# One chunk transposed by DMA, and the stages around it put in another order

## The chip, the cores and the metric

One NeuronCore of a Trainium2 chip. The metric is the device time of one execution in microseconds, as the median of several. Where I say *span*, I mean the time from the first to the last instruction in the profile; the metric is about 1.8 to 2.2 us longer than the span, and that rest is not in the trace.

## The reference, cut to what matters

```python
def _A_ref(x, wqkv, wo):            # sliding window attention, 32 heads of 16, window 8, dilation 2
    qkv = (x @ wqkv)...             # q, k, v
    logits = einsum(q, k[window]) * scale ; attn = softmax(logits)
    o = einsum(attn, v[window])
    return o.reshape(B, S, D) @ wo

def _B_ref(x, w1, w2, w3, w4):      # shifted token mixer and an MLP
    h = gelu(layernorm(x) @ w1)
    x1 = x + shifted(h) @ w2
    return x1 + gelu(layernorm(x1) @ w3) @ w4

xn = layernorm(A_x)                 # S = 2048, D = 512, F = 1376, bf16
out = A_x + _A_ref(xn) * silu(_B_ref(xn))
```

## The kernel before

The 2048 rows are split by parity into two halves of 1024, and each half into two chunks of 512 rows: chunk 0 and 1 are parity 0, chunk 2 and 3 parity 1. Each chunk is normalised on VectorE (DVE), transposed, and then feeds q/k, v and (after a second scaling) w1. `stage_t` transposes half a chunk by TensorE, with a copy out of PSUM (the memory in banks that TensorE writes its results to) behind it; `stage_r` and `stage_m` spread a factor per row over the chunk and multiply it in; `ln_again` makes that factor, with the last step (a power) on GpSimd (POOL). SP is the engine that only issues DMAs, here the *head-row moves* (`spread`), which copy rows of q and k to where the scores read them. The whole order is fixed by hand: each engine executes its instructions in the order in which these calls stand.

```python
    def ln_norm(c):
        p, k = c // 2, c % 2
        x_c = xn[p][:, k * TPC : (k + 1) * TPC, :]
        for lo, hi, mv, rstd in lns[c]:
            for j in range(lo, hi):
                nc.vector.tensor_scalar(
                    out=x_c[:, j, :], in0=x_c[:, j, :], scalar1=mv[:, j - lo, 0:1],
                    scalar2=rstd[:, j - lo : j - lo + 1], op0=ALU.subtract, op1=ALU.mult,
                )

    def ln_again(c):
        r2 = small.tile([P, TPC], F32, name="r2", tag="r2")
        eng = nc.vector if c == 3 else nc.gpsimd
        for lo, hi, mv, rstd in lns[c]:
            r = r2[:, lo:hi]
            eng.tensor_tensor(out=r, in0=rstd, in1=rstd, op=ALU.mult)
            eng.tensor_tensor(out=r, in0=r, in1=mv[:, :, 1], op=ALU.mult)
        eng.tensor_scalar(out=r2, in0=r2, scalar1=EPS, scalar2=None, op0=ALU.add)
        r2b = small.tile([P, TPC], BF16, name="r2b", tag="r2b")
        with nc.allow_low_precision("bf16 factors"):
            nc.gpsimd.tensor_tensor(out=r2b, in0=r2, in1=nhalf, op=ALU.pow)
    ...
    def stage_t(c, h):
        p, k = c // 2, c % 2
        x_c = xn[p][:, k * TPC : (k + 1) * TPC, :]
        pt = pst("wb"[h % 2], "tr_ps").bitcast(BF16)[:, 0, :].rearrange("p (a j q) -> p a j q", a=ND, j=2)
        for j in range(2):
            jj = 2 * h + j
            for dt in range(ND):
                nc.tensor.transpose(pt[:, dt, j, :], x_c[:, jj, dt * P : (dt + 1) * P], ident[:])
        t0 = k * CH + 2 * h * P
        copy = nc.vector.tensor_copy if c == 1 and h else nc.scalar.copy
        copy(out=xnT[p][:, :, t0 : t0 + 2 * P], in_=pt.rearrange("p a j q -> p a (j q)"))
    ...
    def stage_m(c):
        p, k = c // 2, c % 2
        cs = slice(k * CH, (k + 1) * CH)
        rrep = xn2T[c][:, ND - 1, :]
        nc.vector.tensor_tensor(
            out=xn2T[c], in0=xnT[p][:, :, cs], in1=rrep.unsqueeze(1).to_broadcast([P, ND, CH]), op=ALU.mult
        )
```

The order from chunk 2 on, and the attention units of parity 0 with the w2 and q/k tiles between their scores:

```python
    ...
    ln_stats(2)
    ln_again(2)
    stage_w1(0, 1)
    mask_fill(0)
    spread(0, 0, CH)
    ln_norm(2)
    for a in range(2):
        qk_pair(1, a)[0]()
    stage_r(1)
    stage_m(1)
    for a in (2, 3):
        qk_pair(1, a)[0]()
    stage_x()
    stage_t(2, 0)
    stage_t(2, 1)
    ln_stats(3, 0, 2)
    ln_stats(3, 2, 4)
    ln_norm(3)
    ln_again(3)
    stage_w1(1, 0)
    stage_w1(1, 1)
    stage_r(2)
    stage_m(2)
    qk_pair(2, 0)[0]()
    stage_t(3, 0)
    stage_t(3, 1)
    qk_pair(2, 1)[0]()
    stage_w1(2, 0, lambda: stage_r(3))
    stage_m(3)
    mask_fill(1)
    spread(0, CH, X)
    stage_w1(2, 1)
    load_w3()
    stage_w1(3, 0)
    stage_w1(3, 1)
    va = values(0, 0)
    ...
    w2q = [lambda t=t: w2_and(t) for t in range(S // P)]
    qkq = [lambda t=t: qk_one(2 + t // 8, t % 8) for t in range(4, 16)]
    for n, (a, b) in enumerate(
        (("www", "qq"), ("q", "ww"), ("qw", "qw"), ("q", "ww"), ("qw", "qw"), ("q", "ww"), ("qw", "qw"), ("q", "w"))
    ):
        for i, x in enumerate((a, b)):
            for y in x:
                groups[n][i].append((w2q if y == "w" else qkq).pop(0))
    ...
    def attend(n):                  # one attention unit, cut
        prs = [scores(p, u, 0)]     # two PSUM tiles s, t; exp of each on ScalarE
        out = weighted(*prev)       # previous unit: probabilities times values, PSUM tile o
        for f in groups[n][0]: f()  # q/k and w2 tiles, PSUM tiles w, b in turn
        nva = values(*order[n + 1])
        out()                       # DVE casts tile o
        prs.append(scores(p, u, 1))
        for f in groups[n][1]: f()
```

The softmax here doesn't subtract the row's maximum and nothing guards it: scores larger than these inputs give would overflow.

Of the kernel before, what the change touches and what calls it, by code (L numbers as in the profile page):

```python
# [15 lines left out]
def kernel(  # L16
# [14 lines left out]
    nc = tc.nc  # L31
    P = 128
# [11 lines left out]
    CH = 512  # L44
    NCH = S // CH
    TPC = CH // P
# [65 lines left out]
    rr_at = (184, 75)  # L112
    sg_at = (61, 66, B0 + 33.5)

    cnt = {"v": 0, "p": 1, "b": 0, "r": 0, "g": 0}

    def pst(tag, name):
        return psum.tile([P, 2 if tag in "sto" else 1, CH], F32, name=name, tag=tag)
# [114 lines left out]
    def mask_full(w):  # L233
        nc.vector.tensor_tensor(
            out=mask[:, w, :].rearrange("p (g s l) -> p g s l", s=2, l=W),
            in0=gk[:, w, :].rearrange("p (g s) -> p g s", s=2).unsqueeze(3).to_broadcast([P, 32, 2, W]),
            in1=edge[:, w].unsqueeze(1).to_broadcast([P, 32, 2, W]), op=ALU.add,
        )

    def mask_fill(k):  # L240
        for w in range(2):
            for e in range(2):
                for a, b, m in ((0, CH, 0),) if k == 0 else ((CH, CH + 480, 32), (CH + 480, X, 32)):
                    nc.vector.tensor_copy(
                        out=(kT, qT)[w][e][:, :, a:b],
                        in_=mask[:, w, m : m + b - a].unsqueeze(1).to_broadcast([P, ND, b - a]),
                    )

    def spread(p, lo, hi, q=nc.sync, ws=(0, 1)):
        for w in ws:  # L250
            for e in range(2):
                for gr in range(4):
                    r = 32 * gr + DH * e
                    q.dma_start(
                        out=(kT, qT)[w][e][r : r + DH, :, lo:hi], in_=kq[p][w][r : r + DH, :, lo:hi]
                    )
# [32 lines left out]
    lns = {}  # L289

    def ln_stats(c, lo=0, hi=TPC):
        p, k = c // 2, c % 2
        lns.setdefault(c, []).append((lo, hi, *layer_stats(xn[p][:, k * TPC : (k + 1) * TPC, :], "l1", lo, hi)))
# [26 lines left out]
            nc.tensor.transpose(pt[:, dt, :], xn[0][:, j, dt * P : (dt + 1) * P], ident[:])  # L320
        nc.scalar.copy(out=xnT[0][:, :, j * P : (j + 1) * P], in_=pt)  # L321

    def ln_norm(c):
        p, k = c // 2, c % 2
        x_c = xn[p][:, k * TPC : (k + 1) * TPC, :]
        for lo, hi, mv, rstd in lns[c]:
            for j in range(lo, hi):
                nc.vector.tensor_scalar(
                    out=x_c[:, j, :], in0=x_c[:, j, :], scalar1=mv[:, j - lo, 0:1],
# [14 lines that stand above are left out]
        r2s[c] = r2b  # L344
# [9 lines that stand above are left out]
        t0 = k * CH + 2 * h * P  # L354
        copy = nc.vector.tensor_copy if c == 1 and h else nc.scalar.copy
        copy(out=xnT[p][:, :, t0 : t0 + 2 * P], in_=pt.rearrange("p a j q -> p a (j q)"))

    def stage_x():
        nc.gpsimd.tensor_copy(out=xnT[1][:, :, M:X], in_=xnT[0][:, :, M - DW : M])

    def stage_r(c):
        rp = psb("rrep_ps")
        r2 = r2s.pop(c)
        for j in range(TPC):
            nc.tensor.matmul(
                rp[:, j * P : (j + 1) * P], lhsT=r2[:, j : j + 1].to_broadcast([P, P]), rhs=ident[:],
                start=True, stop=True,
            )
        nc.scalar.copy(out=xn2T[c][:, ND - 1, :], in_=rp)
# [8 lines that stand above are left out]
# [4 lines left out]
    def qk_pair(c, a, halves=1):  # L382
        p, k = c // 2, c % 2
        pt = psa("qk_ps")
        w = CH // halves

        def part(hh):
            for b in range(2):
                nt = 2 * a + b
                for dt in range(ND):  # L390
                    nc.tensor.matmul(  # L391
                        pt[:, b, hh * w : (hh + 1) * w], lhsT=wqk_sb[:, dt, nt * P : (nt + 1) * P],
                        rhs=xnT[p][:, dt, k * CH + hh * w : k * CH + (hh + 1) * w],
                        start=(dt == 0), stop=(dt == ND - 1),
                    )
            if hh == halves - 1:
                dst, n0 = qk_dst(p, 2 * a)
                nc.scalar.copy(out=dst[:, n0 : n0 + 2, k * CH : (k + 1) * CH], in_=pt)
                if c == 1:
                    nc.scalar.copy(out=dst[:, n0 : n0 + 2, M:X], in_=pt[:, :, CH - DW : CH])  # L400

        return [lambda hh=hh: part(hh) for hh in range(halves)]
# [13 lines left out]
    def stage_w1(c, a, mid=None):  # L416
        p, k = c // 2, c % 2
        pt = psa("w1_ps")
        for b in range(2):
            g = 2 * a + b  # L420
            if b and mid:
                mid()
            for dt in range(ND):
                nc.tensor.matmul(  # L424
                    pt[:, b, :], lhsT=w1_sb[:, dt, g * P : (g + 1) * P], rhs=xn2T[c][:, dt, :],
                    start=(dt == 0), stop=(dt == ND - 1),
                )
        nc.scalar.activation(
            hT[p][:, 2 * a : 2 * a + 2, 1 + k * CH : 1 + (k + 1) * CH], pt, AF.Gelu_apprx_tanh
        )  # L430
# [100 lines left out]
    def values(p, u):  # L531
        q0, nq, k0, nk = units[u]
        va = v_aug[cnt["v"] % NV]
        cnt["v"] += 1
        vp = psb("v_ps")
        for dt in range(ND):
            nc.tensor.matmul(  # L537
                vp[:nk, :], lhsT=xnT[p][:, dt, k0 : k0 + nk], rhs=wv_sb[:, dt, :],
                start=(dt == 0), stop=(dt == ND - 1),
            )  # L540
        nc.vector.tensor_copy(  # L541
            out=va[:nk, :, 0:DH], in_=vp[:nk, :].rearrange("p (h d) -> p h d", d=DH)
        )
        return va
# [179 lines left out]
    stage_r(0)  # L724
    stage_m(0)
    ln_norm(1)
    mask_full(0)
    mask_full(1)
    parts[1][1]()
    parts[2][1]()  # L730
    qk_pair(0, 3)[0]()
    stage_w1(0, 0)
    stage_t(1, 0)
    stage_t(1, 1)
    ln_stats(2)
    ln_again(2)
    stage_w1(0, 1)
    mask_fill(0)
    spread(0, 0, CH)
    ln_norm(2)  # L740
    for a in range(2):
        qk_pair(1, a)[0]()
    stage_r(1)
    stage_m(1)
    for a in (2, 3):
        qk_pair(1, a)[0]()
    stage_x()
    stage_t(2, 0)
    stage_t(2, 1)
    ln_stats(3, 0, 2)  # L750
    ln_stats(3, 2, 4)
    ln_norm(3)
    ln_again(3)
    stage_w1(1, 0)
    stage_w1(1, 1)
    stage_r(2)
    stage_m(2)
    qk_pair(2, 0)[0]()
    stage_t(3, 0)
    stage_t(3, 1)  # L760
    qk_pair(2, 1)[0]()
    stage_w1(2, 0, lambda: stage_r(3))
    stage_m(3)
    mask_fill(1)
# [1 line left out]
    stage_w1(2, 1)  # L766
    load_w3()
    stage_w1(3, 0)
    stage_w1(3, 1)
    va = values(0, 0)  # L770

    groups = {n: ([], []) for n in range(len(order))}
# [3 lines left out]
        w2_tile(c, j)  # L776

    w2q = [lambda t=t: w2_and(t) for t in range(S // P)]
    qkq = [lambda t=t: qk_one(2 + t // 8, t % 8) for t in range(4, 16)]
    for n, (a, b) in enumerate(  # L780
        (("www", "qq"), ("q", "ww"), ("qw", "qw"), ("q", "ww"), ("qw", "qw"), ("q", "ww"), ("qw", "qw"), ("q", "w"))
    ):
        for i, x in enumerate((a, b)):
            for y in x:
                groups[n][i].append((w2q if y == "w" else qkq).pop(0))
# [8 lines left out]
    st3(2, 2, 3)  # L794
    late[3] += [lambda: ln3_norm(0), lambda: normalise_dn(0, 0), lambda: ln3_turn(0)]
    st3(3, 4)
    st3(4, 5, 6, 7)
    late[6] += [lambda: ln3_norm(1), lambda: normalise_dn(0, 1), lambda: ln3_turn(1)]

    w4s = [w4_tile(t) for t in range(S // P)]  # L800
# [31 lines left out]
    late[N1 + 7].append(lambda: normalise_end(1, 0))  # L832
    CUT = 480
    for w in range(2):
        late[3 + w].append(lambda w=w: spread(1, 0, CUT, nc.gpsimd, (w,)))

    prev = None

# [121 lines left out]
```

## Time and profile before

| | before |
|---|---|
| time, median of 3 | 206.55 us (206.49 to 206.68) |
| span of the profiled run | 204.8 us |
| TensorE busy | 197.3 us, 96% of the span |
| first group of matmuls that takes over 0.1 us too long after 10.4 us | the scores that begin at 50.75 us (0.21 us) |
| sum of the late starts from 43.6 to 90.8 us | 1.85 us |

The lines behind the table stand in the prediction. The last two rows are not in any view: they come from the list of matmul starts in the trace, as the distance from one start to the next less the usual one for its shape (216 ns for 128x512, 56 ns for a transpose, 312 ns from a 128x512 matmul to the first one of the scores). What is late is noted at the start of the group of matmuls that takes too long by it, so 57.74 stands for a group whose successor starts 0.24 us late, at 58.84. Where one engine is busy for 96% of the span, this list is the measure that counts: an engine that looks busy may still start an instruction late, and only a late start is time that a change of order can win.

### The profile page before, as it was taken

How to read it: one execution, taken by the hardware profiler on the slowest of the kernel's cores; microseconds unless marked ns; L12 is line 12 of the kernel's file. 1: busy time of each engine (PE TensorE's matmuls, PEld its weight loads, DVE VectorE, ACT ScalarE, POOL GpSimd, SP SyncE). 2: the span in 40 equal slices, each digit the busy share in tenths (PEclk: the TensorE clock that was granted, in tenths of full speed). 3: DMA queues.
4: the chain of work that ended last, by engine and by line, in shares of the span. 5: the costliest groups of instructions: out<-in, count | busy, mean ns of one | idle time of the engine just before them, and what ended most of it. 6: DMA issues, size and time to landing. Idle time of an engine off the chain costs nothing.

```text
span 204.8 us, 4854 instructions
## 1 busy us (share of the span) xinstructions
PE 197.3 (96%) x1944; PEld 95.6 (47%) x1944; DVE 135.2 (66%) x256; ACT 132.7 (65%) x160; POOL 74.1 (36%) x145
## 2 busy tenths in 40 slices
PE   7799999999999999999999999999999999999990
PEld 2475455444444444544444444444455544444440
DVE  5788996545487986776940001188577968888693
ACT  2366788868968687885556557898788877212130
POOL 4798465000032294933791000003830590700000
PEclk9999999999999999999999999999999999999999
DMA  5992065067900399485779948695130241554312
GB/s 131 361 349 84 15 101 96 0 97 113 293 10 0 108 121 151 86 212 105 180 178 215 286 145 134 93 254 193 34 54 3 52 92 26 122 162 135 95 51 77
DMA packets 30590, 25.69 MB, mean 125 GB/s; under 512 B 12505, under 2 KB 28481, under 8 KB 30569
## 3 DMA queue, kind: packets, MB, share of 16 engines
q1 hardware_dynamic: 28376, 22.17, 43.0%
q0 software_dynamic: 2048, 3.09, 8.9%
q8 instruction: 15, 0.25, 0.5%
q10 hardware_dynamic: 144, 0.13, 0.2%
q14 instruction: 7, 0.05, 0.1%
HBM read 12.40 MB, written 4.46 MB: 82 GB/s over the span
## 4 chain that ended last, share of the span: by engine, by line
PE 87%; ACT 4%; DVE 4%; POOL 1%; DMA 1%; issue 1%
PE w_ps L511 19%; PE w_ps L491 19%; PE qk_ps L391 8%; PE v_ps L537 7%; PE w_ps L424 7%; PE s_ps L557 6%; PE w_ps L447 6%; PE wo_ps L673 6%; PE o_ps L580 4%; PE qk_ps L409 4%; ACT arena L562 3%; PE tr_ps L353 1%; DMA arena<-in_A_x_dram 1%; ACT arena L414 1%; DVE l0s L304 1%; POOL l0r L308 1%
## 5 line engine op out<-in xcount | busy, mean ns | idle before, releaser
L562 ACT ACTIVATE arena<-s_ps 128x960 bf16<-128x960 f32 (+1 forms) x68 | 62.9, 979 | 14.4 <-PE s_ps L557 14.4
L511 PE MATMUL w_ps<-arena 128*128 128x512 bf16 (+1 forms) x164 | 39.1, 380 | 0.0
L496 ACT ACTIVATE arena<-w_ps 128x1024 bf16<-128x1024 f32 x20 | 20.5, 1023 | 15.0 <-PE w_ps L491 14.3
L491 PEld LDWEIGHTS <-arena 128*128 128x128 bf16 (+1 forms) x176 | 17.5, 100 | 20.6 <-issue 0.4
L622 POOL DMA_DIRECT2D arena<-orw x48 | 24.9, 527 | 5.8 <-DVE orw L592 5.8
L511 PEld LDWEIGHTS <-arena 128*128 128x128 bf16 (+1 forms) x176 | 16.5, 98 | 19.6
L683 POOL TENSOR_TENSOR arena<-arena 128x512 bf16<-128x512 bf16 x6 | 7.7, 1301 | 44.5 <-DVE arena L681 44.5
L526 ACT ACTIVATE sig<-arena 128x512 bf16<-128x512 bf16 x16 | 10.1, 630 | 20.8 <-DVE arena L517 20.7
L541 DVE CAST v_aug<-v_ps 128x512 bf16<-128x512 f32 x17 | 11.7, 688 | 14.6 <-PE v_ps L537 14.6
L592 DVE CAST orw<-o_ps 128x960 bf16<-128x960 f32 (+1 forms) x17 | 19.7, 1156 | 2.5 <-PE o_ps L580 2.4
L491 PE MATMUL w_ps<-arena 128*128 128x512 bf16 (+1 forms) x88 | 19.5, 379 | 0.1
L491 PE MATMUL w_ps<-arena,arena 128*128 128x512 bf16 (+1 forms) x88 | 19.2, 379 | 0.0
L391 PE MATMUL qk_ps<-arena 128*128 128x512 bf16 (+1 forms) x104 | 18.6, 330 | 0.5 <-ACT arena L321 0.5
L537 PE MATMUL v_ps<-wv_sb,arena 128*128 128x512 bf16 x68 | 17.5, 380 | 0.1
L557 PEld LDWEIGHTS <-arena 32*128 32x128 bf16 x544 | 10.1, 92 | 14.5 <-issue 14.4
L273 POOL TENSOR_SCALAR l3r<-l3m 128x1 f32<-128x1 f32 (+1 forms) x10 | 2.2, 222 | 39.0 <-DVE l3m L282 39.0
L557 PE MATMUL s_ps<-arena 32*128 32x120 bf16 (+1 forms) x544 | 15.8, 214 | 0.0
L447 PE MATMUL w_ps<-arena 128*128 128x512 bf16 x64 | 15.7, 380 | 0.1
L517 DVE TENSOR_TENSOR arena<-w_ps,arena 128x512 bf16<-128x512 f32 x16 | 11.0, 686 | 7.2 <-PE w_ps L511 7.2
L650 DVE TENSOR_TENSOR arena<-arena,orw 128x1440 bf16<-128x1440 bf16 (+1 forms) x2 | 1.6, 784 | 20.5 <-DMA orw<-rden_d 20.5
L424 PE MATMUL w_ps<-arena 128*128 128x512 bf16 x64 | 14.6, 379 | 0.0
L451 DVE TENSOR_TENSOR arena<-w_ps,arena 128x512 bf16<-128x512 f32 x16 | 10.7, 686 | 4.1 <-PE w_ps L447 4.1
(98 smaller groups left out, 278.9 us busy)
## 6 DMA issues: line engine op xcount, KB each, us to landing
x1n_dram<-arena SPq DMA_DIRECT2D x4, 512.0 KB, 3.0
arena<-in_A_x_dram SPq DMA_DIRECT2D x4, 512.0 KB, 6.1
arena<-in_A_x_dram SPq DMA_DIRECT2D x6, 256.0 KB, 7.0
out_dram<-arena SPq DMA_DIRECT2D x6, 256.0 KB, 3.0
arena<-in_B_w_dram SPq DMA_DIRECT2D x1, 1376.0 KB
arena<-in_B_w_dram SPq DMA_DIRECT2D x1, 1280.0 KB
arena<-arena SPq DMA_DIRECT2D x16, 72.0 KB, 2.6
arena<-arena SPq DMA_DIRECT2D x16, 68.0 KB, 3.5
```

Of the source, the lines that this page charges most:

```text
L391: nc.tensor.matmul(pt[:, b, hh * w : (hh + 1) * w], lhsT=wqk_sb[:, dt, nt * P : (nt + 1) * P], rhs=xnT[p][:, dt, k * CH + hh * w : k * CH ...
L424: nc.tensor.matmul(pt[:, b, :], lhsT=w1_sb[:, dt, g * P : (g + 1) * P], rhs=xn2T[c][:, dt, :], start=(dt == 0), stop=(dt == ND - 1),)
L447: nc.tensor.matmul(pt, lhsT=w2_src(p, g, m0), rhs=w2_sb[:, g, :], start=(g == 0), stop=(g == ND - 1))
L491: nc.tensor.matmul(pt[:fs, ft % 2, :], lhsT=w3_sb[:, dt, ft * P : ft * P + fs], rhs=x1nT[c][:, dt, :], start=(dt == 0), stop=(dt == ND - 1),)
L496: nc.scalar.activation(h3(c, 2 * a, 2), pt, AF.Gelu_apprx_tanh)
L511: nc.tensor.matmul(pt, lhsT=h3(c, ft, 1)[:fs, 0, jj * P : (jj + 1) * P], rhs=w4_sb[:fs, ft, :], start=(ft == 0), stop=(ft == NF - 1),)
L537: nc.tensor.matmul(vp[:nk, :], lhsT=xnT[p][:, dt, k0 : k0 + nk], rhs=wv_sb[:, dt, :], start=(dt == 0), stop=(dt == ND - 1),)
L557: nc.tensor.matmul(st[:nk, b, i * nq : (i + 1) * nq], lhsT=kT[e][r : r + 32, dt, k0 : k0 + nk], rhs=qT[e][r : r + 32, dt, q0 : q0 + nq], s ...
L562: nc.scalar.activation(prv[:nk, 2 * h : 2 * h + 2], st[:nk, :, 0 : 4 * nq], AF.Exp, scale=SCALE)
L592: nc.vector.tensor_copy(out=orw[p, r][:, :, :, q0 - ra : q0 - ra + nq], in_=op[:, :, 0 : 4 * nq].rearrange("p j (s q) -> p j s q", q=nq),)
L622: nc.gpsimd.dma_start(out=oT[p][DH * hh : DH * (hh + 1), :, ra : ra + rw], in_=orw[p, r][32 * cg : 32 * cg + DH, jj],)
L673: nc.tensor.matmul(pt, lhsT=oT[p][:, dt, i * P : (i + 1) * P], rhs=wo_sb[:, dt, :], start=(dt == 0), stop=(dt == ND - 1),)
```

## The change

Intent: take chunk 2's transposes off TensorE by sending the chunk to DRAM and back through a DMA transpose; norm chunk 3 in halves so that its own transposes can fill the time until the data is back; issue the moves of head rows of parity 0 in parts, so that SP's queue is free for the store and the transpose; load ScalarE's exp table before the first scores; and take three q/k tiles out of the attention units so that these become alike. Cut to its core:

```diff
+    def turn_dma(c, lo=0, hi=TPC):
+        p, k = c // 2, c % 2
+        rows = x1n_dram[c * CH + lo * P : c * CH + hi * P, :]
+        nc.sync.dma_start(
+            out=rows.rearrange("(i q) d -> q i d", q=P), in_=xn[p][:, k * TPC + lo : k * TPC + hi, :]
+        )
+        return lambda: nc.sync.dma_start_transpose(
+            out=xnT[p][:, :, k * CH + lo * P : k * CH + hi * P], in_=rows
+        )
...
     ln_norm(1)
-    mask_full(0)
-    mask_full(1)
     parts[1][1]()
     parts[2][1]()
     qk_pair(0, 3)[0]()
+    ln_stats(2, 0, 2)
     stage_w1(0, 0)
     stage_t(1, 0)
     stage_t(1, 1)
-    ln_stats(2)
+    ln_stats(2, 2, 4)
+    mask_full(0)
+    ln_norm(2)
+    turn_dma(2)()
     ln_again(2)
     stage_w1(0, 1)
-    mask_fill(0)
-    spread(0, 0, CH)
-    ln_norm(2)
+    mask_full(1)
+    mask_fill(0, (0,))
     for a in range(2):
         qk_pair(1, a)[0]()
     stage_r(1)
     stage_m(1)
+    ln_stats(3, 0, 2)
+    spread(0, 0, CH, nc.sync, (0,))
     for a in (2, 3):
         qk_pair(1, a)[0]()
     stage_x()
-    stage_t(2, 0)
-    stage_t(2, 1)
-    ln_stats(3, 0, 2)
     ln_stats(3, 2, 4)
-    ln_norm(3)
-    ln_again(3)
+    ln_norm(3, slice(0, 1))
     stage_w1(1, 0)
     stage_w1(1, 1)
     stage_r(2)
+    stage_t(3, 0)
+    ln_norm(3, slice(1, 2))
     stage_m(2)
+    ln_again(3)
     qk_pair(2, 0)[0]()
-    stage_t(3, 0)
     stage_t(3, 1)
     qk_pair(2, 1)[0]()
+    mask_fill(0, (1,))
+    spread(0, 0, CH, nc.sync, (1,))
     stage_w1(2, 0, lambda: stage_r(3))
...
     stage_w1(3, 0)
+    qk_pair(2, 2)[0]()
     stage_w1(3, 1)
+    qk_one(2, 6)
+    nc.scalar.preload_act_table_set("exp_and_others")
     va = values(0, 0)
...
-    qkq = [lambda t=t: qk_one(2 + t // 8, t % 8) for t in range(4, 16)]
+    qkq = [lambda t=t: qk_one(2 + t // 8, t % 8) for t in range(7, 16)]
     for n, (a, b) in enumerate(
-        (("www", "qq"), ("q", "ww"), ("qw", "qw"), ("q", "ww"), ("qw", "qw"), ("q", "ww"), ("qw", "qw"), ("q", "w"))
+        [("www", "qw")] + [("q", "ww")] * 6 + [("q", "q")]
     ):
```

Left out: the parameters that let `ln_norm`, `mask_fill` and `spread` do a part; the start of the PSUM rotation (`"p": 0` for 1, since one more tile is taken); one statistics step moved a unit on; and the second head-row move of parity 1, one attention unit later (unit 5 for unit 4).

More of the change, by code (lines that the diff above doesn't have):

```diff
@@ L113 @@
     sg_at = (61, 66, B0 + 33.5)
-    cnt = {"v": 0, "p": 1, "b": 0, "r": 0, "g": 0}
+    cnt = {"v": 0, "p": 0, "b": 0, "r": 0, "g": 0}
     def pst(tag, name):
@@ L238, in mask_full, with mask_fill @@
         )
-    def mask_fill(k):
-        for w in range(2):
+    def mask_fill(k, ws=(0, 1)):
+        for w in ws:
             for e in range(2):
@@ L247, in mask_fill, with spread @@
                     )
-    def spread(p, lo, hi, q=nc.sync, ws=(0, 1)):
+    def spread(p, lo, hi, q=nc.sync, ws=(0, 1), es=(0, 1)):
         for w in ws:
-            for e in range(2):
+            for e in es:
                 for gr in range(4):
@@ L321, in first_t, with ln_norm @@
         nc.scalar.copy(out=xnT[0][:, :, j * P : (j + 1) * P], in_=pt)
-    def ln_norm(c):
+    def ln_norm(c, part=slice(None)):
         p, k = c // 2, c % 2
         x_c = xn[p][:, k * TPC : (k + 1) * TPC, :]
-        for lo, hi, mv, rstd in lns[c]:
+        for lo, hi, mv, rstd in lns[c][part]:
             for j in range(lo, hi):
@@ L796 @@
     st3(3, 4)
-    st3(4, 5, 6, 7)
+    st3(4, 5, 6)
+    st3(5, 7)
     late[6] += [lambda: ln3_norm(1), lambda: normalise_dn(0, 1), lambda: ln3_turn(1)]
@@ L834 @@
     for w in range(2):
-        late[3 + w].append(lambda w=w: spread(1, 0, CUT, nc.gpsimd, (w,)))
+        late[3 + 2 * w].append(lambda w=w: spread(1, 0, CUT, nc.gpsimd, (w,)))
     prev = None
```

## The prediction

> **What bounds the kernel now.** I read the page first: who is busy, and when.
>
> ```profile
> PE 197.3 (96%) x1944; PEld 95.6 (47%) x1944; DVE 135.2 (66%) x256; ACT 132.7 (65%) x160; POOL 74.1 (36%) x145
> PE   7799999999999999999999999999999999999990
> PEclk9999999999999999999999999999999999999999
> PE 87%; ACT 4%; DVE 4%; POOL 1%; DMA 1%; issue 1%
> ```
>
> TensorE is busy from the third slice to the last but one, at full granted clock; every other engine has a third of its time free. Busy matmuls can hide waits, so next I took the matmul starts from the trace and read the distance from each to the next. A 128x512 matmul takes 216 ns, a transpose 56 ns, in nearly every case. From 10.4 us to 43.6 us not one matmul starts late: the two load stages before it and the tail after 198.1 us, both untouched by the change, are the only large holes. Then the chain of waits in order of time (start, duration, what), around the three chunks that are still transposed by TensorE:
>
> ```profile
> 17.98 0.89 PE tr_ps L353 x16
> ...
> 27.73 0.89 PE tr_ps L353 x16
> 28.62 3.45 PE w_ps L424 x16
> 32.08 0.22 PE rrep_ps L365 x4
> 32.30 1.73 PE qk_ps L391 x8
> 34.03 0.89 PE tr_ps L353 x16
> ```
>
> The line at 27.73 is chunk 2: 16 transposes back to back, 0.89 us, on the path. The 1.73 at 32.30 is the first reader of the transposed chunk.
>
> From 43.6 us to 90.8 us (the first eight attention units beside the w2 and q/k tiles) there are small stalls. Beyond the normal slots I count: 0.21 at 50.75, 0.14 at 53.70, 0.24 at 57.74, about 0.17 each at 61.97, 67.02, 73.00, 78.05 and 84.03, 0.05 and 0.07 at 68.96 and 79.97, 0.29 at 87.25; 1.85 us in all. The ScalarE timeline there:
>
> ```profile
> 45.05 1.28 ACT L562 ACT_TABLE_LOAD   x1 [0.15 <-PE s_ps L557]
> 46.35 1.94 ACT L562 ACTIVATE arena<-s_ps 128x1024 bf16<-128x1024 f32 x2
> 49.00 1.94 ACT L562 ACTIVATE arena<-s_ps 128x1024 bf16<-128x1024 f32 x2 [0.72 <-PE s_ps L557]
> 50.83 1.08 ACT L414 CAST arena<-qk_ps 128x512 bf16<-128x512 f32 x2
> 51.77 1.88 ACT L562 ACTIVATE arena<-s_ps 128x960 bf16<-128x960 f32 x2
> ```
>
> The exp table load does not stall TensorE: ScalarE still idles 0.72 us before the second pair of exps. What backs ScalarE up a little is the pair of q/k casts at 50.83.
>
> **What the skill says.** "TensorE: Matmul & The Clock Gate", Part 4, gives a 128x128 bf16 transpose about 390 ns alone and about 275 ns in one kernel. This trace disagrees: 16 of them leave every 56 ns, so chunk 2 costs 0.89 us and not 4.4, and I use 0.89. "DMA: Bandwidth & Descriptors", DMA Transpose (X-bar), says a DMA transpose needs HWDGE and an SBUF destination, and that two streams of them at once corrupt each other; the before kernel sends four, all from SP, and the new one joins that queue, so it is legal. "ScalarE: Activation LUTs", What ACT_TABLE_LOAD costs, has 1283 ns plus a drain of 1380 ns; the trace shows the 1283 ns, but exp starts 0.02 us after the load ends, so I count no drain. "SBUF — State Buffer" says DVE and GpSimd share a port pair by an exclusive lock; the trace agrees in kind: the same 128x2 tensor_scalar on POOL takes 0.23 us at 13.21 and 1.20 us at 14.24, when DVE runs the 128x2048 multiply.
>
> **The change, part by part.**
>
> *Chunk 2 by DMA.* Removes 16 transposes: -0.89 us on the path, and two 128x1024 copies (about 1 us each) from ScalarE, which is not the bound there. It adds a 512 KB store and a DMA transpose. Both have rows in the before kernel:
>
> ```profile
> 69.22 0.40 SPq L473 DMA_DIRECT2D x1n_dram<-arena  x1
> 69.72 0.62 SPq L614 DMA_DIRECT2D dn<-den_d  x1
> 72.21 2.63 SPq L478 DMA_TRANSPOSE arena<-x1n_dram  x1
> DMA to landing us min/median/max: 4.3/4.6/5.0
> ```
>
> 3.0 us for the store, 4.3 to 5.0 for the transpose, 7.3 to 8.0 together. When can it start? DVE ends the norm of chunk 1 at 17.0; two stats pairs of 1.6 us with the 0.7 us copy of chunk 1 between them end near 21.1; POOL is free of its memset at 20.4 and needs 0.23 + 0.73 us per half for the rstd, the second half slowed by the lock; the four norms (1.4 us) end at 23.8 to 24.3. It lands at 31.1 to 32.3, estimated from those rows. The first reader comes at 32.14 in matmul starts, less 0.89, plus 0.45 for the half of chunk 3's transposes now ahead of it: 31.70. So the landing straddles the need; I put 0.2 us of stall there (0 to 0.8).
>
> *Norm of chunk 3 in halves.* No work added. It lets transposes of half 0 go ahead of q/k, which buys the DMA the 0.45 us above. DVE: the multiply of chunk 1 can start at 25.8 (ScalarE's cast of the factors) and must end by 27.57, when w1 of chunk 1 starts; I estimate 27.0 to 27.3. Then two stats pairs, and half 0's norm ends near 31.2 against 31.25. The factor of chunk 3 needs POOL's power (1.04 to 1.85 us) after DVE at about 34.8, while DVE now fills masks beside it: ready at 35.9 to 37.1, needed at about 36.5 to 36.7. I put 0.2 us for all of these.
>
> *Head-row moves in parts.* 32 SP issues of about 0.6 us, the same number; only their times move. Part 1 is behind the transpose, to about 34.6 us; part 2 starts after its fill at about 36, takes 8 x 0.645 = 5.2 us to issue and lands near 43.7. First scores: 44.57 - 0.89 + 1.73 + 0.86 (three q/k tiles moved ahead) = 46.3. Some 2.5 us to spare: nothing.
>
> *Tiles and the table.* Three q/k tiles leave the attention units for the stage before: the same 12 matmuls, 2.6 us either way. The later units become alike (one q/k tile, then two w2 tiles). The stalls at 57.74, 68.96 and 79.97 are values waiting for the bank of a q/k tile whose cast sits behind two exps; with no w2 tile between, these 0.36 us go, and the 0.14 at 53.70 too as only one cast is behind the first unit. The 0.17 before each next unit's scores stays: two 216 ns x 4 groups (1.83 us) are shorter than two exps (1.83 us plus start), and one unit that had none will get it. Net -0.33. The table load moves into the shadow of values: first exp some 0.7 us nearer to its scores, worth 0 on the path.
>
> Sum: -0.89 + 0.2 + 0.2 - 0.33 = -0.82; 206.55 becomes about 205.7. I shade it to 205.6, since the halves look placed on purpose to avoid just these stalls.
>
> **Rivals.** (1) *The DMA lands late.* The path norm, store, transpose has no slack by my count, and each us past 31.7 is a us on TensorE. For: the before run shows 5.0 us under traffic. Against: the input loads have all landed by 17.3 us in the trace, and SP's moves are queued behind it, so the engines are empty. At 1.5 us late: 206.9. (2) *All hidden, everything in time.* Then 0.89 and 0.33 are both kept, plus perhaps some of the 0.17s: 205.3, at best 204.8. (3) *ScalarE becomes the bound in the attention units*, through one cast per unit: 2 x 1.83 + 0.59 = 4.3 us against 5.05 us of TensorE. Against it: that ratio; the time would not move by more than 0.3. (4) *The DMA transpose frees nothing since TensorE waits for DVE anyway*: against it, the slots show no wait from 10.4 to 43.6.
>
> **Range and chances.** Gains are capped by 0.89 + 1.85 us, which would be 203.8 with every stall gone; 2% would be 202.4, so faster by 2% needs work that the change does not remove. Slower by 2% needs 4 us of lateness in a path that I estimate at most 1 or 2 us late. Range 204.8 to 206.5.
>
> **What would show it right or wrong.** After: 32 transposes at the stage's line in place of 48; store issued at 23.5 to 24.5 us and transpose landed by 31.1 to 32.3; a TensorE gap under 0.8 us before the first q/k of chunk 2, small ones before the factor matmuls of chunk 3; w3 starting about 0.8 us earlier than 88.41; span after w3 unchanged. The prediction is wrong if the transpose takes much over 5 us, if the norm of chunk 2 ends after 25 us, if the moves of part 2 land after the first scores, or if the stalls between units grow.

## The result, and the profile after

Ratios in this document are the mean time of one kernel's fast runs over that of the other's of the same rounds, so not quite the ratio of the medians that stand beside them.

| | before | after |
|---|---|---|
| time, median of 6 | 206.57 us (206.49 to 206.68) | 206.01 us (205.92 to 206.29) |
| ratio | | 0.9974 (95%: 0.9962 to 0.9987) |
| span of the profiled run | 204.8 us | 204.1 us |

The change makes the kernel 0.54 us faster (0.0026 x 206.57), a quarter of a per cent. The page of the kernel after, by engine, by slice and by the chain:

```profile
PE 195.2 (96%) x1900; PEld 94.9 (47%) x1928; DVE 135.0 (66%) x256; ACT 131.5 (64%) x157; POOL 74.5 (37%) x149
PE   7899999999999999999999999999999999999990
PE 71%; DVE 11%; DMA 9%; issue 3%; POOL 3%; ACT 2%; SPq 0%; DVEq 0%; POOLq 0%
```

TensorE is still busy for 96% of a span that is a little shorter. Two things here mislead. The count of matmuls fell by 44 where the change removes 16: the weight loads fell by exactly 16 (from 1944 to 1928), so 28 matmul records are missing, and the busy time of this line is low by a little. And the share of TensorE in the chain fell from 87% to 71% although nothing changed behind 87.73 us: the last stage takes 72.29 us in both kernels. At the end the chain now runs back over DMAs that landed at nearly the same time as the work beside them. A chain is one path, and where two are about as long, which of them is shown is chance.

What did change stands in SP's queue and in the chain from 31 us on. SP's timeline of the kernel after (start, duration, what):

```profile
23.29 0.39 SPq L361 DMA_DIRECT2D x1n_dram<-arena  x1
26.28 1.41 SPq L364 DMA_TRANSPOSE arena<-x1n_dram  x1
27.81 23.05 SPq L254 DMA_DIRECT2D arena<-arena  x32
```

The store goes out at 23.29 us, the transpose 2.99 us later, when the store has landed. The last of the transpose's completion records is at 31.11 us, 4.83 us after its issue; the first q/k of chunk 2 starts at 31.49 us. So the DMA is in time, by 0.38 us. The chain of the kernel after, next:

```profile
32.62 1.22 DVE arena L385
34.63 0.44 issue
35.07 1.58 POOL r2b L343
36.70 0.40 PE rrep_ps L375 x4
37.09 4.10 PE w_ps L434 x19
```

Here the chain leaves TensorE. The four matmuls at 36.70 spread the factors of chunk 3, and they wait for POOL's power, which starts at 35.07 and takes 1.58 us. By the list of starts they come 0.44 us late; the profile of before has no such gap.

A table of stages tells the rest. Stage 1 runs from the first transpose of chunk 1 (17.6 to 17.9 us) to the first scores, stage 2 from there to the first w3 matmul, stage 3 (38.72 us in every kernel) over w3, stage 4 from the first scores of parity 1 to the last matmul. Where the three q/k tiles are moved, I put their 12 matmuls (12 x 0.216 = 2.59 us) back into stage 2, so that all rows compare.

| kernel | stage 1 | stage 2 | stage 4 | mean span of the fast runs | time less span |
|---|---|---|---|---|---|
| before | 26.76 | 43.84 | 72.29 | 204.76 | 1.78 |
| after | 26.31 | 43.80 | 72.29 | 204.18 | 1.86 |
| e1 front only | 26.32 | 43.83 | 72.58 | 204.52 | 2.03 |
| e2 tiles only | 26.76 | 43.48 | 72.29 | 204.38 | 2.14 |
| e3 no preload | 26.31 | 43.80 | 72.29 | 204.32 | 1.85 |
| e4 again first | 25.86 | 43.80 | 72.29 | 203.98 | 1.87 |
| e5 turn on PE | 27.21 | 43.48 | 72.29 | 204.80 | 2.24 |
| e6 late norm | 26.96 | 43.80 | 72.29 | 204.90 | 1.87 |
| e7 no half ahead | 26.31 | 43.79 | 72.29 | 204.26 | 1.85 |
| e8 split w2 | 25.86 | 47.15 | 72.30 | 207.25 | 1.87 |
| e9 ACT plus 2 | 26.31 | 43.49 | 72.29 | 203.83 | 1.88 |
| e10 ACT plus 1 | 26.31 | 43.49 | 72.59 | 204.08 | 1.85 |
| e11 split, late cast | 25.86 | 43.65 | 72.29 | 203.57 | 1.84 |
| e12 e4 and e9 | 25.86 | 43.49 | 72.29 | 203.48 | 1.88 |

Stages are from the profiled execution of each kernel, and they repeat to 0.01 us between kernels that share the code, which makes them a finer measure than the time. Stage 1 gained 0.45 us, and stage 2, where I had counted on 0.33, gained 0.04.

### The profile page after: what moved, and what is told of

Same layout as the page of the kernel before. It is cut to its first block, busy times and chain, and to the rows that moved or that the text cites. A ratio compares the mean times of both kernels' runs of the same rounds, so it can differ in the third digit from the quotient of the medians.

```text
span 204.1 us, 4800 instructions
## 1 busy us (share of the span) xinstructions
PE 195.2 (96%) x1900; PEld 94.9 (47%) x1928; DVE 135.0 (66%) x256; ACT 131.5 (64%) x157; POOL 74.5 (37%) x149
## 4 chain that ended last, share of the span: by engine, by line
PE 71%; DVE 11%; DMA 9%; issue 3%; POOL 3%; ACT 2%; SPq 0%; DVEq 0%; POOLq 0%
PE w_ps L501 19%; PE w_ps L521 10%; PE v_ps L547 8%; PE s_ps L567 7%; PE w_ps L457 6%; PE qk_ps L401 5%; PE w_ps L434 5%; PE o_ps L590 4%; PE qk_ps L419 4%; DMA den_d<-orw 3%; PE wo_ps L683 3%; DMA arena<-rden_d 2%; DVE arena L537 2%; DMA rden_d<-rb 1%; DVE arena L691 1%
## 5 line engine op out<-in xcount | busy, mean ns | idle before, releaser
L521 PE MATMUL w_ps<-arena 128*128 128x512 bf16 (+1 forms) x156 | 38.5, 380 | 0.6 <-issue 0.2
L401 PE MATMUL qk_ps<-arena 128*128 128x512 bf16 (+1 forms) x109 | 20.4, 332 | 0.5 <-ACT arena L321 0.3
L501 PE MATMUL w_ps<-arena 128*128 128x512 bf16 (+1 forms) x86 | 19.4, 379 | 0.2
L527 DVE TENSOR_TENSOR arena<-w_ps,arena 128x512 bf16<-128x512 f32 x16 | 11.0, 686 | 7.9 <-PE w_ps L521 7.9
L457 PE MATMUL w_ps<-arena 128*128 128x512 bf16 x63 | 15.2, 380 | 0.1
L434 PE MATMUL w_ps<-arena 128*128 128x512 bf16 x63 | 14.6, 379 | 0.0
L401 PEld LDWEIGHTS <-arena 128*128 128x128 bf16 x112 | 10.6, 98 | 7.9 <-DMA arena<-in_A_wqkv_dram 0.8
```

Source lines behind the costliest of these rows:

```text
L401: nc.tensor.matmul(pt[:, b, hh * w : (hh + 1) * w], lhsT=wqk_sb[:, dt, nt * P : (nt + 1) * P], rhs=xnT[p][:, dt, k * CH + hh * w : k * CH ...
L434: nc.tensor.matmul(pt[:, b, :], lhsT=w1_sb[:, dt, g * P : (g + 1) * P], rhs=xn2T[c][:, dt, :], start=(dt == 0), stop=(dt == ND - 1),)
L457: nc.tensor.matmul(pt, lhsT=w2_src(p, g, m0), rhs=w2_sb[:, g, :], start=(g == 0), stop=(g == ND - 1))
L501: nc.tensor.matmul(pt[:fs, ft % 2, :], lhsT=w3_sb[:, dt, ft * P : ft * P + fs], rhs=x1nT[c][:, dt, :], start=(dt == 0), stop=(dt == ND - 1),)
L521: nc.tensor.matmul(pt, lhsT=h3(c, ft, 1)[:fs, 0, jj * P : (jj + 1) * P], rhs=w4_sb[:fs, ft, :], start=(ft == 0), stop=(ft == NF - 1),)
```

## The experiments

All twelve gave correct results, and each has four to six timed runs beside the kernel before (206.54 to 206.61 us there).

### e1: the front of the change alone

The kernel after with the loop, the q/k tiles, the table load and the PSUM start of before.

```diff
-    qk_pair(2, 2)[0]()
     stage_w1(3, 1)
-    qk_one(2, 6)
-    nc.scalar.preload_act_table_set("exp_and_others")
...
+        (("www", "qq"), ("q", "ww"), ("qw", "qw"), ...            # the loop of before
```

> Front part of the change alone (chunk 2 by DMA, norm of chunk 3 in halves, head-row moves in parts); q/k tiles, exp table and loop as in the kernel before. Theory T (read from the trace after): 0.89 us of transposes gone, 0.44 us given back at the factor matmuls of chunk 3, the DMA itself in time: -0.45 us against before, about 206.1. Rival R1 (the front keeps its full 0.89 and the loss is elsewhere): 205.7. Rival R2 (the gain comes from tiles and table, the front is a wash): 206.5.

Measured: 206.57 us, ratio 0.9999 (0.9986 to 1.0013). The time did not move, but stage 1 is 26.32 us, 0.44 less than before, as Theory T had it. Two things ate it: stage 4 is 0.29 us longer (e10 comes back to that), and 0.25 us more lies outside the span (2.03 against 1.78).

### e2: tiles and table alone

The opposite half: the kernel before with the moved tiles, the early table and the new loop.

> Moved q/k tiles, early exp table and the regular loop alone, chunk 2 still transposed on TensorE. Theory T (the stalls of the attention units sum to 1.76 us after against 1.85 us before): -0.1 us against before, about 206.45. The prediction's term: -0.33, about 206.2. Rival R2: -0.5, about 206.0.

Measured: 206.45 us, ratio 1.0000 (0.9987 to 1.0012). Stage 2 is 43.48 us: 0.36 us less than before, the prediction's term and not the one that I had read from the trace after. In the time it does not show, since 0.36 us more lies outside the span. By mean spans the halves nearly add up: -0.24 (e1) and -0.38 (e2) against -0.57 for the whole. That is luck: e1 loses 0.29 us in stage 4, which the whole does not, and the whole has 43.80 us in stage 2: with the front in place, 0.32 us of this half are lost again.

### e3: without the early table

```diff
-    nc.scalar.preload_act_table_set("exp_and_others")
```

> The changed kernel without the early exp table; the load then happens at the first exp. Theory T: ScalarE has over 1 us free before the second pair of exps in the first unit, so the same time as after within 0.1 us. Rival (the load sits on the path): up to 1.28 us slower than after.

Measured: 206.15 us, ratio 0.9983 (0.9970 to 0.9995); all stages as after. ScalarE's timeline, first of the kernel after, then of e3:

```profile
46.48 1.28 ACT L785 ACT_TABLE_LOAD   x1
47.77 1.94 ACT L572 ACTIVATE arena<-s_ps 128x1024 bf16<-128x1024 f32 x2
50.95 1.94 ACT L572 ACTIVATE arena<-s_ps 128x1024 bf16<-128x1024 f32 x2 [1.24 <-PE s_ps L567]
```

```profile
47.11 1.28 ACT L572 ACT_TABLE_LOAD   x1 [0.54 <-PE s_ps L567]
48.41 1.94 ACT L572 ACTIVATE arena<-s_ps 128x1024 bf16<-128x1024 f32 x2
51.06 1.94 ACT L572 ACTIVATE arena<-s_ps 128x1024 bf16<-128x1024 f32 x2 [0.72 <-PE s_ps L567]
```

The early load brings the first exp forward by 0.53 us (0.64, less 0.11 by which the whole run of e3 is later), and ScalarE's idle time before the second pair grows by as much, from 0.72 to 1.24 us. The load was hidden before, and hiding it better is worth nothing.

### e4: the factors of chunk 3 first

```diff
-    stage_m(2)
     ln_again(3)
+    stage_m(2)
```

> The changed kernel with the factors of chunk 3 computed on DVE before the multiply of chunk 2, so that POOL's power is not held up behind DVE's multiply and mask fills. Theory T (the 0.44 us TensorE gap in front of the factor matmuls of chunk 3 is this wait and nothing else takes its place): 0.3 to 0.45 us faster than after, about 205.6. Rival: POOL is blocked by DVE's mask fills just as long, or w1 of chunk 2 then waits for its later multiply: no change.

Measured: 205.80 us, ratio 0.9967 (0.9955 to 0.9980); stage 1 is 25.86 us, 0.45 less than after. TensorE's timeline of the kernel after, then POOL's of the same kernel:

```profile
35.39 1.03 PE L434 MATMUL w_ps<-arena 128*128 128x512 bf16 x4
36.70 0.40 PE L375 MATMUL rrep_ps<-ident,r2b 128*128 128x128 bf16 x4 [0.28 <-POOL r2b L343]
```

```profile
35.07 1.57 POOL L343 TENSOR_TENSOR r2b<-r,nhalf 128x4 bf16<-128x4 f32 x1 [3.84 <-DVE r L340]
```

The same two of e4:

```profile
35.65 1.03 PE L434 MATMUL w_ps<-arena 128*128 128x512 bf16 x4
36.52 0.39 PE L375 MATMUL rrep_ps<-ident,r2b 128*128 128x128 bf16 x4
```

```profile
33.48 1.90 POOL L343 TENSOR_TENSOR r2b<-r,nhalf 128x4 bf16<-128x4 f32 x1 [1.99 <-DVE r L340]
```

In e4 the power is done at 35.38 us, over a microsecond early, and four w1 matmuls and the factor matmuls follow without a gap (35.65 + 4 x 0.216 = 36.51). It even takes longer there, 1.90 us; it starts while DVE's multiply runs, and whether that is the reason was not tested. So the gap after is the power's late start: in the changed order DVE makes its input only behind the multiply of chunk 2. (POOL starts 0.49 us after DVE's last step ended, in e4 0.48, where DVE's mask fills do not run yet; so nothing shows that the fills set that start.)

### e5: chunk 2 on TensorE again

```diff
-    turn_dma(2)()
...
     stage_x()
+    stage_t(2, 0)
+    stage_t(2, 1)
```

> The changed kernel with chunk 2 transposed by TensorE again, all else as after. Theory T: +0.89 us of transposes, but the factor matmuls of chunk 3 come 0.89 us later and their 0.44 us wait goes: +0.45 us against after, about 206.45. Rival R1 (the transposes cost their full time): +0.89, about 206.9. Rival (the transposes were hidden): 0.

Measured: 207.05 us, ratio 1.0023 (1.0010 to 1.0035). Stage 1 is 27.21 us, 0.90 more than after: Rival R1. The wait before the factor matmuls of chunk 3 did not go. TensorE's timeline of e5, the same two lines as in e4:

```profile
36.37 1.03 PE L434 MATMUL w_ps<-arena 128*128 128x512 bf16 x4
37.67 0.40 PE L375 MATMUL rrep_ps<-ident,r2b 128*128 128x128 bf16 x4 [0.28 <-POOL r2b L343]
```

From 36.37 to 37.67 are 1.30 us, as from 35.39 to 36.70 in after: 0.44 more than four matmuls take. The transposes stand ahead of the factor matmuls of chunk 2, and behind those runs the path that the wait ends: ScalarE's cast, DVE's multiply (at 33.59 us for 32.62), DVE's input of the power, the power (at 36.04 for 35.07). All of it moves with TensorE, so the wait keeps its length. My reading that the transposes' removal had *brought* this wait was wrong: it belongs to the order of `stage_m` and `ln_again`, and it costs the same with the transposes and without. The DMA is worth its full 0.90 us in this order. (Stage 2 is 0.32 us shorter here, and 0.38 us more lies outside the span than after.)

### e6: the DMA 1.5 us later

```diff
-    ln_norm(2)
-    turn_dma(2)()
-    ln_again(2)
-    stage_w1(0, 1)
     mask_full(1)
     mask_fill(0, (0,))
+    ln_norm(2)
+    turn_dma(2)()
+    ln_again(2)
+    stage_w1(0, 1)
```

> The changed kernel with the second mask table and the first fill (0.68 + 1.29 us of DVE) put ahead of the norm of chunk 2, so that its store and DMA transpose start about 2 us later. The transpose landed at 31.1 us after and was needed at 31.5. Theory T (slack of 0.4 us): TensorE waits about 1.6 us before the first q/k of chunk 2, less the 0.44 us of the later wait: +1.1 to +1.6 us against after. Rival (the DMA has much slack, or DVE's and POOL's order shifts the rest): under +0.3.

Measured: 206.75 us, ratio 1.0009 (0.9997 to 1.0022); stage 1 is 0.65 us longer than after. The store goes out at 24.79 us, 1.50 us later and not 2, since the norm now runs without a wait for POOL in its middle. TensorE's timeline of e6:

```profile
31.12 0.61 PE L353 MATMUL tr_ps<-ident,arena 128*128 128x128 bf16 x8
32.67 1.89 PE L401 MATMUL qk_ps<-arena 128*128 128x512 bf16 x7 [0.94 <-ACT arena L379]
36.57 1.03 PE L434 MATMUL w_ps<-arena 128*128 128x512 bf16 x4
37.43 0.39 PE L375 MATMUL rrep_ps<-ident,r2b 128*128 128x128 bf16 x4
```

The eight transposes end their slots at 31.12 + 0.45 = 31.57, and q/k starts at 32.67: 1.10 us late. The named releaser (a ScalarE cast, of the factors of chunk 2) is not what it waited for: in after the same q/k starts at 31.49 us, before this cast, which begins at 32.01 there. The transpose's last completion record is at 32.53 us, 1.42 us later than after. Against TensorE's own stream, which runs 0.08 us later as a whole in this run, that is 1.34 us later; less the 1.10 of waiting it leaves 0.24 us of slack. After has 0.38 us between record and start, and here a start follows its record by 0.14 us: 0.24 again. And since the factor matmuls now come later than the power, their 0.44 us are gone (36.57 + 0.86 = 37.43): 1.10 - 0.44 = 0.66, measured 0.65. That lies between the two expectations: Theory T had the mechanism, but a delay of 2 us for 1.50. Its slack of 0.4 us was nearer to 0.24.

### e7: no half of chunk 3 ahead

```diff
     stage_r(2)
-    stage_t(3, 0)
     ln_norm(3, slice(1, 2))
     stage_m(2)
     ln_again(3)
     qk_pair(2, 0)[0]()
+    stage_t(3, 0)
     stage_t(3, 1)
```

> The changed kernel with half 0 of chunk 3 transposed after the first q/k of chunk 2 instead of ahead of it. The first q/k would then want its data at 31.05 us, and the DMA lands at 31.1. Theory T: a wait of 0.1 to 0.3 us there, part of it taken out of the later 0.44 us: 0 to +0.2 us against after. Rival (the half ahead is worth its 0.45 us): +0.45.

Measured: 206.12 us, ratio 0.9977 (0.9965 to 0.9990); stage 1 as after. The first q/k starts at 31.30 us where its slot was at 31.09: 0.21 us late, and the wait before the factor matmuls is shorter by the same 0.21. In this kernel the half ahead buys nothing, since a later wait takes it back. Without that wait (e4's order) it was not tried.

### e8: w2 tiles split around the scores

The order of e4, and in units 1 to 6 one w2 tile in two halves of two matmuls, the first before the second scores, the second behind them, then the q/k tile and the other w2 tile.

```diff
+        if n in mids:
+            mids[n]()                       # w2_tile(..., 0, 2)
         if out and n < N1:
             out()
         prs.append(scores(p, u, 1))
...
-        [("www", "qw")] + [("q", "ww")] * 6 + [("q", "q")]
+        [("www", "qw")] + [("", "qw")] * 6 + [("q", "q")]     # with w2_tile(..., 2, 4) ahead of "qw"
```

> The order of e4, and one w2 tile of each later unit split in two halves around its second scores, with the q/k tile after them, so that both gaps between scores are about 2 us. Theory T (the 0.17 us before each unit's scores is TensorE waiting for the second of two exps, 1.83 us plus start, behind 1.83 us of matmuls): six or seven of them go, 0.9 to 1.2 us faster than e4, about 204.6. Rival (ScalarE or DVE backs up elsewhere, or each extra change of tile shape costs 0.1 us): no gain over e4.

Measured: 209.11 us, ratio 1.0127 (1.0112 to 1.0143): 3.3 us slower than e4. The waits before the first scores of the units are gone (0.34 us from scores to the next group in place of 0.51; the second scores now take 0.41), which fits a wait for exp. But TensorE's timeline has a new one in each unit:

```profile
62.64 1.02 PE L461 MATMUL w_ps<-arena 128*128 128x512 bf16 x4 [0.54 <-DVE arena L467]
```

The second w2 tile wants the PSUM bank of the split one, whose add on DVE stands behind the 1.15 us cast of the attention output.

### e9 and e10: two, and one, tiny copies on ScalarE

What of the 0.32 us that stage 2 lost with the front in place? In the kernels after, e3, e4, e6 and e7 ScalarE's wait for the third unit's second scores ends, and the exp behind it starts 0.31 us later than in other units. It is always behind the 63rd record of ScalarE's stream (counted in the trace itself, with the semaphore records that the views leave out), and 1.0 us after it an 8192-byte packet stands on the instruction queue. So I moved the stream.

```diff
+    pad = small.tile([P, 4], F32, name="pad", tag="pad", bufs=1)
+    for i in range(2):                      # e10: range(1)
+        nc.scalar.copy(out=pad[:, i : i + 1], in_=nhalf[:, i : i + 1])
     mask_tables()
```

> The changed kernel with two tiny ScalarE copies (128x1) at the start, where ScalarE is idle; nothing else. In five kernels of this order ScalarE answers 0.31 us late at the same record of its stream (the 63rd), 1.0 us before an 8192-byte packet on the instruction queue, and TensorE then waits 0.32 us in the third attention unit; the two kernels with two more ScalarE instructions ahead do not show it. Theory T (the hiccup sits at a fixed place of the instruction stream, and moving the stream by two hides it behind a running exp): the stage from the first scores to w3 goes from 41.21 to 40.89 us, span 0.32 us shorter than after. Rival (it belongs to the data flow of that unit): 41.21 and no change.

> The same with one tiny copy. Theory T: the place moves by one; in the third unit it falls on a record that waits anyway, so that stage is 40.89 us, but the next such place (about 128 records on) falls where it fell in the kernel with the front part alone, which lost 0.29 us at 153 to 155 us: the last stage goes from 72.29 to about 72.58 us, and the span is that of after within 0.1 us. Rival (data flow): 41.21 and 72.29.

Measured: e9 205.77 us, ratio 0.9958 (0.9945 to 0.9970); e10 206.03 us, ratio 0.9966 (0.9952 to 0.9980). Stages 2 and 4: 43.49 and 72.29 us in e9, 43.49 and 72.59 in e10 (in the expectations stage 2 is counted without the moved 2.59 us, so 40.90 there). Both as Theory T had them, to 0.01 us. ScalarE's timeline of the kernel after in the third unit, then TensorE's:

```profile
60.03 0.59 ACT L424 CAST arena<-qk_ps 128x512 bf16<-128x512 f32 x1
61.44 1.83 ACT L572 ACTIVATE arena<-s_ps 128x960 bf16<-128x960 f32 x2 [0.82 <-PE s_ps L567]
```

```profile
62.82 0.89 PE L567 MATMUL s_ps<-arena 32*128 32x120 bf16 x16
```

The same two of e9:

```profile
60.16 0.59 ACT L424 CAST arena<-qk_ps 128x512 bf16<-128x512 f32 x1
61.26 1.83 ACT L572 ACTIVATE arena<-s_ps 128x960 bf16<-128x960 f32 x2 [0.51 <-PE s_ps L567]
```

```profile
62.95 0.58 PE L567 MATMUL s_ps<-arena 32*128 32x120 bf16 x16
```

0.82 us idle against 0.51, and the next scores 0.89 us against 0.58. Two copies of one element per partition, at the start of the kernel, take 0.31 us off TensorE. With one copy instead, the third unit is as in e9, and the pause shows behind the 191st record, 128 on. ScalarE's timeline of e10 there, then of e9 at the same place:

```profile
153.14 1.83 ACT L572 ACTIVATE arena<-s_ps 128x960 bf16<-128x960 f32 x2 [0.92 <-PE s_ps L567]
```

```profile
152.72 1.83 ACT L572 ACTIVATE arena<-s_ps 128x960 bf16<-128x960 f32 x2 [0.62 <-PE s_ps L567]
```

That is also where e1 lost its 0.29 us: its stream has as many ScalarE records (250) as e10's. Shown is that the pause sits at a fixed count of records, at two places 128 apart, and costs only where ScalarE is idle there and TensorE waits for it. That it is the change to the next block of instructions is an inference from the packet beside it.

### e11: the split again, with the cast moved

```diff
-        if out and n < N1:
+        if out and n < N1 and n not in mids:
             out()
...
-        for f in groups[n][1]:
+        for i, f in enumerate(groups[n][1]):
             f()
+            if n in mids and i == 0:
+                out()
```

> The split of w2 tiles as in e8, with DVE's cast of the attention output moved behind the add of the split tile. In e8 the waits before scores were gone (0.34 us in place of 0.51), but TensorE waited 0.5 to 0.8 us per unit for the PSUM bank of the split tile, whose add stood behind that cast. Theory T: both waits are gone; the stage from the first scores to w3 falls from 41.21 us to 39.9 to 40.4 us, time about 204.7 to 205.1. Rival (DVE, at 4.7 us of work for a unit of 4.9 us, is the bound in these units): no better than e4.

Measured: 205.43 us, ratio 0.9944 (0.9930 to 0.9957). Stage 2 is 43.65 us (41.06 without the moved tiles): 0.15 less than e4's, where I had expected 0.8 or more. TensorE's list of starts shows why it is little: the second scores now wait 0.08 us and the second w2 tile 0.08 us in nearly every unit, about as much as the 0.17 that went, and in one unit the q/k tile comes 0.41 us late, at 71.2 us, since DVE has the norm of the first chunk (1.37 us) in front of the cast that frees its bank. DVE is near its limit in these units, and the split moves the wait to it.

### e12: e4 and e9 together

```diff
+    pad = ...                               # as e9
...
-    stage_m(2)
     ln_again(3)
+    stage_m(2)
```

> The two findings together: factors of chunk 3 ahead of the multiply of chunk 2 (e4) and two tiny ScalarE copies at the start (e9). If they are independent, the stages are 28.45, 40.90, 38.72 and 72.29 us, 0.76 us less than after, about 205.3 us. If one takes the other's place, 205.7 to 205.8.

Measured: 205.27 us, ratio 0.9943 (0.9929 to 0.9956). The stages are 25.86, 43.49, 38.72 and 72.29 us (28.45 and 40.90 as the expectation counts them), each as expected. The two findings are independent, and this is the fastest kernel with e11: 1.2 us faster than before (0.0057 x 206.57), more than twice the change's own gain, by one line moved and two idle copies on top of the change.

## Why the prediction was right or wrong

The time, 206.01 us, lies in the range of 204.8 to 206.5, which is wide beside the gain: predicted were 205.6, that is 0.95 us for the 0.54 measured. The mechanism of the terms was right, and of the sum's four terms three were mis-sized. Two of these misses, 0.2 us too much for the DMA and 0.24 too little for the waits around chunk 3, cancel by luck; the third, 0.29 us at the attention units, is most of what is left of the sum's miss (-0.49 in stages for -0.82).

- *Transposes: -0.89.* Right. e5 puts them back and stage 1 grows by 0.90 us. I took 56 ns a piece from the trace and not the page's 275 ns, with which the term would have been 4.4 us. But the page did not disagree with the trace, as I wrote: its figure is how long one transpose takes, and 56 ns is the distance between two starts. One record of a transpose lasts 219 ns in this trace (its end is modelled).
- *DMA late: +0.2 (0 to 0.8).* It was 0: landed 31.11, needed 31.49 us. The estimate of the landing (31.1 to 32.3) held at its early end, as the norm ended in time for a store at 23.29 where I had 23.8 to 24.3. That the path has hardly any slack was right: 0.24 us by e6.
- *The waits around chunk 3: +0.2.* It was 0.44, all of it in the step that I had named (POOL's power behind DVE, ready at 35.9 to 37.1; it came at 36.65). I spread 0.2 us over several waits by the middle of each estimate; the one that had the least slack took it all. e4 shows it by removing it. That this wait is no price of the DMA, as I came to think on reading the trace after, is e5's result.
- *Units made alike: -0.33.* The mechanism gives -0.36 (e2; -0.35 in e9), and in both kernels' lists of starts values no longer wait for the bank of a q/k tile (0.24, 0.07 and 0.05 us in before). But the kernel after has -0.04: a pause of ScalarE that no view of the profile before shows on the path fell into the third unit. This is the failed step: I summed waits by their cause in the data flow and had no term for one whose place depends on the count of instructions ahead.
- *Table: 0.* Right (e3). *Head-row moves: 0.* Nothing contradicts it: no stage shows a wait for them, and no run moved them alone. The last move of part 2 is issued at 39.86 us, well ahead of the first scores at 46.52.

In stages the sum is -0.89 + 0.44 - 0.04 = -0.49 us, and -0.54 was measured by the ratio. What stays open is the time outside the span. It is 1.78 us in before, 1.84 to 1.88 in ten of the others, and 2.03 to 2.24 in e1, e2 and e5, in nearly all of their runs. It hid e2's gain in the time, and together with the pause that of e1, and I found nothing in the traces that tells what it is.

Of the rivals, *the DMA lands late* became true as soon as e6 delayed it; *all hidden* would have been right for e12 (205.27 against the 205.3 that I gave it), which takes both waits away; *ScalarE becomes the bound* did not come true: the waits for exp of about 0.17 us a unit are those of before, and only the pause was added; that *TensorE waits for DVE anyway* is refuted by e5's 0.90 us.

## What to carry to other kernels

When one engine is busy for nearly the whole span, list its late starts, name each one's cause, and sum them: once the pause was known, that predicted the stages of e9, e10 and e12 to 0.01 us, while the sum in the prediction, which lacked it, was 0.33 us off. A single wait with no slack is worth more care than the mean of several. Before you credit or blame a part of a change for a few tenths of a microsecond, run each part alone and compare stages between fixed marks in the trace as well as the whole time: halves of this change looked like nothing on the clock and were worth 0.4 us each in their stage. And look for waits that sit at a fixed count of instructions: a no-op ahead of them may move them to where they cost nothing, or back.

## What the Trainium skill lacked or had wrong

- "TensorE: Matmul & The Clock Gate", Part 4, has about 390 ns alone and about 275 ns in one kernel for a 128x128 bf16 transpose. That is the time of one; the section lacks what a row of them costs. In a row they start every 56 ns here (with 219 ns for one record), and 16 of them cost 0.90 us (e5).
- "ScalarE: Activation LUTs", What ACT_TABLE_LOAD costs, adds a drain of about 1380 ns to the load's 1283. The load takes 1.28 us in these runs and exp starts 0.01 to 0.02 us after it; no drain shows.
- "Runtime: NRT & Kernel Launch", Instruction fetch mechanics, has instructions refilled in 16 KiB blocks of 256 and the crossing of a block mostly hidden. On this core one instruction queue moves packets of 16384 bytes (15 in the kernel after, q8 of its page), but the packets beside ScalarE's pauses are on the other (q14) and have 8192 bytes, and the pauses are 128 records apart. They are not always hidden: 0.29 to 0.32 us on TensorE's path in the kernel after, e1 and e10, if the pause is this fetch, as the packet suggests.
- No page tells that the time between the span and the measured time differs between builds of nearly the same kernel: 1.78 us in before, 2.24 us in e5. What it is made of, these runs do not show.
